# A re-ordered step table for chunked attention followed by a phase-mixing layer, on one core

## The chip, the core and the metric

The kernel runs on one core of a Trainium2 chip. The time is the device time of one execution in microseconds (us), the median over the runs; the profile is one profiled execution of the same program, with its span from the first to the last instruction. The engines are named as the profile names them: PE is TensorE, DVE is VectorE, ACT is ScalarE, POOL is GpSimd and SP is SyncE. PEld is the weight-load half of PE.

## What is computed

Eight batch elements, each of 8 heads, 576 rows and 64 columns per head, go through two stages.

```python
# 1: attention inside chunks of 64 rows
scores = scale * q_c @ k_c.T;  attn = softmax(scores);  x = attn @ v_c      # x: 8 x 576 x 512
# 2: phase mixing and a channel layer
theta = x @ w_theta
zr, zi = x * cos(theta), x * sin(theta)
y = w_tok_r @ zr + w_tok_i @ zi          # over the 576 rows
u = x + y
out = u + relu(u @ w_ch)
```

Inputs and output are float32; inside, the operands of PE are float16 and the sums float32.

## The kernel before, in words

The eight batch elements are worked in four pairs p = 0 to 3. A pair has five groups: A and B are rows 0 to 255 and 256 to 511 of its first element, C and D the same of its second, and M the last 64 rows of both, one in each half of the partitions. A, B, C and D hold two tiles of 128 rows each, M one. A pair thus has nine tiles j = 0 to 8 (A: 0, 1; B: 2, 3; C: 4, 5; D: 6, 7; M: 8).

The work is cut into 562 steps, and the table ORDER writes their order out by hand; every engine executes its own instructions in exactly that order, and waits where an operand or a buffer isn't there yet. A step is named by its kind, the pair and the group or tile, and the buffer or bank that it takes: `S.2B.6` makes the scores of pair 2, group B, in the PSUM bank 6 and the one behind it. The kinds that matter here, with their lines:

- `qk`, `v`, `lw`, `lp`, `lc` are loads, nearly all issued by POOL (L174, L179, L233, L243, L246, L249). They also turn float32 into float16.
- `T`, `Tq`, `Tk` turn q and k on DVE (L286); `S` is the score product on PE (64 small matmuls for a group of two tiles, 32 for M, L325); `E` is the exponential on ACT (L355); `V0`, `V1` are the two halves of the value product on PE (16 small matmuls each, 8 for M, L389); `N0`, `N1` divide by the row sums on DVE (L404, L406).
- `X` transposes x on PE (L421); `xa`, `xv`, `xd` bring it to SBUF by ACT, by DVE, or do the whole transposing by a DMA on SP's queue (L433); `H` is theta on PE (L449); `G` takes cosine and sine on ACT (L471, L472), with a table load (L152) where the exponential was before; `Z` multiplies on DVE (L498, L499).
- `Y` is the token mixing, nine matmuls of 512 columns for a tile on PE (L528); `Ya`, `Yb`, `Ym` are its parts; for the second element of a pair the parts need `Z` of C, of D and of M. `A` adds x on DVE (L550). `U` with `ua` or `uv`, or the DMA `ud` (L563), transposes u. `W` is the channel product on PE (L573), `R` the relu and add on DVE (L578), `st`, `sa`, `sg` are the stores from SP's, ACT's and POOL's queue. `dm` is a filler product of zeros.

The score product uses PE in quarters of 32 rows, the value product in halves of 64; the others use the full array. `crossed(p, g)` says for which groups the second tile's two chunks change sides between the score's rows and the halves of PSUM; `load_v` puts the rows of v where the value product then expects them.

```python
def crossed(p, g):
    return int(p > 0 or g not in "AB")
```

The bank and buffer numbers in the table matter as well: a step that takes a bank waits until the reader of what was in it is done.

Of the kernel before, what the change touches and what calls it, by code (L numbers as in the profile page):

```python
# [23 lines left out]
Z0.0B Ya.01.6 Yb.01 TW.02.4 twa.02 Z.0M Ym.01 T.1M.2 A.01 Yb.03 V0.0C.0 Ym.03 V1.0C.4 Tq.0D.1
S.1M.6 E.1M.4 Ya.02.7 Yb.02 Ym.02 N1.0C Tk.0D S.0D.4 N0.0C A.03 TW.00.0 qk.1B.2 A.02 X.0C.3
lw.04.0 E.0D.3 U.01.6 ua.01.0 U.02.4 ua.02.1 U.03.5 twv.00 Ya.00.0 V1.0D.6 uv.03.2 qk.1A.6
xv.0C.1 N1.0D V0.0D.4 H.0C.2 G.0C.1 qk.1D.3 V0.1M.6 N0.0D X.0D.4 xv.0D.3 v.1B N0.1M Z.0C Yb.00
v.1A Ym.00 v.1D H.0D.4 Ya.05.2 T.1B.4 G.0D.5 V1.1M.3 A.00 Ya.06.6 TW.04.0 S.1B.4 Ya.04.7 N1.1M
X.1M.3 E.1B.4 Z.0D Yb.06 T.1A.4 Ym.06 S.1A.4 qk.1C.6 A.06 Yb.05 T.1D.5 xv.1M.3 U.06.6 twv.04
E.1A.1 Ym.05 Ya.07.4 V1.1B.0 qk.2M.3 A.05 ua.06.3 N1.1B V0.1B.5 N0.1B Yb.04 lc.00 S.1D.2 v.1C  # L30
V1.1A.0 Yb.07 qk.2C.5 Ym.07 qk.2D.4 N1.1A E.1D.2 V0.1D.2 N0.1D X.1B.0 xa.1B.4 V1.1D.5 Ym.04
H.1M.1 H.1B.2 qk.2B.0 N1.1D V0.1A.5 A.07 qk.2A.2 qk.3B.1 Y.08.4 T.1C.7 A.04 N0.1A X.1A.5 U.04.6
G.1M.2 Z.1M xv.1A.1 U.00.7 S.1C.0 v.2M G.1B.6 E.1C.4 A.08 X.1D.5 xv.1D.2 v.2B W.06.2 R.06.3
U.07.0 H.1A.4 uv.04.3 V0.1C.2 v.3D uv.07.4 v.2A uv.00.5 W.00.7 G.1A.7 N0.1C U.05.0 U.08.6
uv.08.5 v.2C V1.1C.2 W.01.1 uv.05.6 H.1D.4 N1.1C X.1C.2 Z.1A Z.1B R.01.2 qk.3A.6 W.08.3 xa.1C.4
Y.10.0 H.1C.1 G.1D.7 Z.1D T.2M.8 T.2A.7 W.02.4 S.2M.5 v.3B G.1C.9 Z.1C R.02.4 E.2M.1 Y.13.6 A.13
T.2B.9 S.2A.1 W.04.4 R.00.0 Y.16.5 qk.3D.0 R.04.5 R.08.6 W.05.4 S.2B.6 T.2D.7 E.2B.7 T.2C.2
Y.11.3 A.11 R.05.8 A.16 W.03.6 R.03.9 Y.15.7 A.15 E.2A.10 V1.2A.5 A.10 S.2C.3 E.2C.11 V0.2M.1
N0.2M V1.2M.7 N1.2M Y.14.2 N1.2A V0.2B.3 N0.2B V0.2A.0 V0.2C.6 v.2D Y.17.5 A.14 A.17 V1.2C.2
N1.2C N0.2A N0.2C Y.18.4 xd.2C.12 S.2D.2 st.04 qk.3M.2 V1.2B.0 E.2D.1 X.2A.5 W.07.6 N1.2B v.3C  # L40
V0.2D.0 R.07.7 N0.2D V1.2D.2 xa.2A.11 v.3A X.2M.7 X.2B.5 v.3M Y.12.6 A.12 N1.2D H.2A.0 xa.2M.10
A.18 T.3A.7 H.2M.6 xa.2B.1 G.2M.13 T.3D.5 Z.2M H.2C.4 H.2B.6 G.2A.6 xd.2D.5 ud.16.4 G.2C.0 Z.2C
ud.17.2 T.3B.9 H.2D.0 W.17.4 S.3D.2 G.2D.4 Z.2D ud.11.6 W.11.5 R.17.5 R.11.13 sa.06 ud.14.3
W.16.0 st.08 qk.3C.8 T.3M.4 Y.25.1 T.3C.1 Y.24.5 Y.27.4 A.24 ud.13.1 G.2B.5 S.3B.5 A.25 W.14.1
R.14.3 Y.26.7 Z.2A S.3M.1 E.3B.6 E.3D.1 V1.3D.2 R.16.12 S.3C.5 A.27 Z.2B sa.07 ud.15.2 ud.12.6
ud.10.4 ud.18.5 W.18.0 E.3C.10 E.3M.7 Y.20.4 sa.17 A.26 V0.3M.7 R.18.11 V0.3C.0 N1.3D W.15.5
R.15.5 N0.3C st.14 S.3A.2 E.3A.3 W.12.6 Y.23.5 V1.3M.2 A.20 N0.3M N1.3M W.10.7 st.11 R.10.7
sa.10 R.12.13 V0.3D.3 N0.3D V1.3C.1 ud.25.3 N1.3C Y.28.0 W.13.4 st.16 ud.27.0 V1.3A.2 V0.3B.6
A.28 st.18 R.13.7 N1.3A Y.21.0 A.21 st.02 ud.24.2 Y.22.2 A.22 xd.3M.12 H.3M.0 V1.3B.3 sa.03
W.24.2 N0.3B N1.3B V0.3A.6 N0.3A ud.20.1 G.3M.10 W.25.1 xd.3D.9 H.3D.3 G.3D.7 xd.3C.1 Z.3M  # L50
H.3C.6 G.3C.5 Z.3D A.23 Z.3C ud.21.4 xd.3B.6 W.21.0 ud.22.3 sa.05 H.3B.3 G.3B.7 Z.3B ud.26.2
W.22.6 st.12 Y.34.7 R.25.8 W.26.3 R.24.6 sg.25 R.22.13 Y.35.1 A.35 R.26.1 R.21.8 xd.3A.10 W.27.6
W.20.2 H.3A.3 sg.21 st.01 st.00 Y.36.0 Y.37.1 R.20.0 sa.20 A.34 ud.28.4 W.28.7 ud.23.6 G.3A.7
A.36 Z.3A Y1.31.0 sa.13 Y.38.3 ud.34.3 A.37 ud.35.1 R.28.7 A1.31 st.24 A.38 W.34.0 Y0.31.7 A0.31
sg.22 ud.37.0 W.37.3 W.35.7 R.34.13 R.37.6 st.26 Y.32.0 A.32 U0.31.3 uv0.31.1 R.35.1 U1.31.1
Y.33.4 A.33 st.15 ud.36.4 W.36.7 W.23.3 R.27.5 ud.38.2 sg.35 sa.34 R.23.13 R.36.1 W.38.6 R.38.0
sa.37 sa.28 Y.30.4 Wp.31.6.7 uv1.31 sa.38 A.30 W0.31 ud.32.3 W.32.1 R0.31.7 sa0.31 R.32.6 U.30.6
sa.36 W1.31 uv.30.1 R1.31 st.27 ud.33.6 W.33.4 R.33.0 st.32 sa.33 W.30.6 sg.23 dm.2.7 R.30.13
st1.31 sa.30
""".split()  # L60


@with_exitstack
def kernel(
# [150 lines left out]
    def crossed(p, g):  # L215

        return int(p > 0 or g not in "AB")
# [64 lines left out]
    def size(g):  # L282
        return 1 if g == "M" else 2
# [464 lines left out]
```

## Time and profile before

| | |
|---|---|
| time, median of 3 runs | 194.83 us |
| all runs | 194.83, 194.02, 199.41 us |
| profiled execution: span from first to last instruction | 191.7 us |
| PE busy | 173.9 us (91%) |
| DVE busy | 138.8 us (72%) |
| ACT busy | 81.4 us (42%) |
| POOL busy | 88.4 us (46%) |
| DMA | 31.86 MB, mean 166 GB/s |

The profiled execution has no time of its own beside its span; the median of the runs lies 3.1 us above the span, the fastest run 2.3 us.

A busy engine is one with an instruction in flight; times count from the start of the span. PE's timeline lists when each matmul starts, so the distance from one start to the next tells what a matmul costs while others follow, and a longer distance than usual is a wait or a change between kinds of matmul. A row of the waits names who waited for whom, the total, how often, and the longest.

### The profile page before, as it was taken

To read this page: it belongs to the slowest core of one execution; us is meant where nothing else is said; L and a number is where in the kernel's file an instruction comes from. 1 tells how busy PE (TensorE), PEld (TensorE's weight loads), DVE (VectorE), ACT (ScalarE), POOL (GpSimd) and SP (SyncE) were. 2 spreads that over 40 slices of the span, in tenths; PEclk is the share of its full clock that TensorE was granted. 3 is DMA by queue.
4 is the path that set the end of the run, shared out by engine and by line. 5 is a ranking of instruction groups with operands and counts; after the bars stand their busy time and mean duration, and the time that the engine had idled before them with its cause. 6 is when DMAs were issued, how large, how long until landed. Compare 5 with 4: busy or idle time off the path is not lost.

```text
span 191.7 us, 5957 instructions
## 1 busy us (share of the span) xinstructions
PE 173.9 (91%) x2579; PEld 91.1 (48%) x2579; DVE 138.8 (72%) x255; ACT 81.4 (42%) x100; POOL 88.4 (46%) x125
## 2 busy tenths in 40 slices
PE   0168899999999999999999969999999999999992
PEld 0155455645554655554555425454444444455450
DVE  0564789879779977996885968396686677553782
ACT  3113895476629946803218659142032560400000
POOL 8998289697798955799878000000000001100110
PEclk9999999999999999999999999999999999999999
DMA  5999999999999999999999986497356894885667
GB/s 159 202 157 182 188 132 143 164 177 165 151 153 183 175 182 181 157 116 152 164 133 132 196 145 168 82 197 222 74 158 126 112 281 103 246 230 150 180 173 259
DMA packets 103338, 31.86 MB, mean 166 GB/s; under 512 B 94672, under 2 KB 99152, under 8 KB 103312
## 3 DMA queue, kind: packets, MB, share of 16 engines
q0 software_dynamic: 76048, 17.33, 98.2%
q1 hardware_dynamic: 23872, 9.57, 23.9%
q10 hardware_dynamic: 3392, 4.59, 7.6%
q8 instruction: 20, 0.33, 0.7%
q14 instruction: 6, 0.05, 0.1%
HBM read 33.06 MB, written 9.44 MB: 222 GB/s over the span
## 4 chain that ended last, share of the span: by engine, by line
PE 78%; DMA 8%; DVE 4%; POOL 4%; issue 2%; ACT 1%; DVEq 0%; ACTq 0%; POOLq 0%
PE psum L528 35%; PE psum L573 14%; PE psum L449 12%; PE psum L325 6%; PE psum L389 5%; DMA out_dram<-mid 3%; PE psum L421 3%; DMA mid<-x 2%; DMA v<-in_v_dram 2%; PE psum L264 1%; POOL big L174 1%; PE psum L555 1%; POOL big L179 1%; DVE mid L578 1%; DVE x L406 1%
## 5 line engine op out<-in xcount | busy, mean ns | idle before, releaser
L528 PE MATMUL psum<-zr,wT 128*128 128x512 f16 (+2 forms) x185 | 62.6, 375 | 0.1
L528 PE MATMUL psum<-zi,wT 128*128 128x512 f16 (+2 forms) x184 | 59.6, 374 | 0.0
L528 PEld LDWEIGHTS <-wT 128*128 128x128 f16 (+1 forms) x369 | 31.3, 100 | 32.9 <-issue 0.5
L233 POOL DMA_DIRECT2D v<-in_v_dram x54 | 41.0, 787 | 10.1 <-DMA big<-in_k_dram 4.5
L672 POOL DMA_DIRECT2D out_dram<-mid x5 | 2.7, 551 | 75.3 <-DVE mid L578 75.3
L573 PE MATMUL psum<-wch,uT 128*128 128x512 f16 x140 | 35.1, 380 | 0.0
L550 DVE TENSOR_TENSOR x<-psum,x 128x512 f16<-128x512 f32 x35 | 23.7, 683 | 15.3 <-PE psum L528 15.1
L449 PE MATMUL psum<-wtheta,mid 128*128 128x512 f16 x144 | 33.2, 379 | 1.7 <-DMA mid<-x 1.7
L355 ACT ACTIVATE mid<-psum 128x1024 f16<-128x1024 f32 (+1 forms) x19 | 17.3, 930 | 33.9 <-PE psum L325 32.2
L578 DVE SCALAR_TENSOR_TENSOR mid<-psum,x 128x512 f32<-128x512 f32 (+1 forms) x37 | 23.9, 669 | 7.7 <-PE psum L573 5.6
L406 DVE TENSOR_TENSOR x<-psum,recip 128x512 f16<-128x512 f32 (+1 forms) x40 | 25.5, 638 | 1.4
L286 DVE STREAM_TRANSPOSE big<-big 128x1024 f32<-128x1024 f32 (+3 forms) x25 | 24.7, 1011 | 1.3 <-DMA big<-in_q_dram 0.9
L325 PE MATMUL psum<-big 32*64 32x64 f16 x1152 | 15.3, 199 | 9.5 <-DVE big L286 9.5
L471 ACT ACTIVATE big<-psum,pihalf 128x1024 f16<-128x1024 f32 x14 | 15.6, 1116 | 17.4 <-PE psum L449 17.4
L449 PEld LDWEIGHTS <-mid 128*128 128x128 f16 x144 | 13.9, 98 | 18.1 <-DMA mid<-x 2.2
L325 PEld LDWEIGHTS <-big 32*64 32x64 f16 x1152 | 13.0, 112 | 15.1 <-DVE big L286 10.1
L573 PEld LDWEIGHTS <-uT 128*128 128x128 f16 x140 | 12.4, 98 | 13.4 <-issue 0.8
L152 ACT ACT_TABLE_LOAD x12 | 15.4, 1283 | 6.3 <-DVE recip L404 4.8
L179 POOL DMA_DIRECT2D big<-in_q_dram x15 | 13.8, 920 | 1.7 <-DMA big<-in_k_dram 0.9
L472 ACT ACTIVATE big<-psum 128x1024 f16<-128x1024 f32 x14 | 14.3, 1024 | 0.0
L389 PEld LDWEIGHTS <-mid 64*64 64x64 f16 x576 | 8.9, 113 | 11.4 <-issue 9.0
L389 PE MATMUL psum<-v,mid 64*64 64x65 f16 x576 | 12.2, 202 | 2.0 <-DMA v<-in_v_dram 1.3
(51 smaller groups left out, 135.7 us busy)
## 6 DMA issues: line engine op xcount, KB each, us to landing
big<-in_q_dram POOLq DMA_DIRECT2D x15, 256.0 KB, 6.5
big<-in_k_dram POOLq DMA_DIRECT2D x15, 256.0 KB, 7.0
out_dram<-mid SPq DMA_DIRECT2D x13, 256.0 KB, 2.8
out_dram<-mid ACTq DMA_DIRECT2D x13, 256.0 KB, 3.0
v<-in_v_dram POOLq DMA_DIRECT2D x18, 128.0 KB, 5.7
v<-in_v_dram POOLq DMA_DIRECT2D x36, 64.0 KB, 6.1
out_dram<-mid POOLq DMA_DIRECT2D x5, 256.0 KB, 3.1
out_dram<-mid SPq DMA_DIRECT2D x5, 128.0 KB, 3.0
```

The source lines that it names most:

```text
L179: nc.gpsimd.dma_start(t[:, w].rearrange("p h s d -> p h (s d)"), ap[2 * p + bb, :, s0 : s0 + GT, :].rearrange("h (p s) d -> p h (s d)", s=2),)
L233: nc.gpsimd.dma_start(v16[rows, slot + t, :, 0:D], v[b, :, t0 : t0 + m, :].rearrange("h s d -> s h d"),)
L286: nc.vector.transpose(out.bitcast(FP32).rearrange("p (x l s) -> p x s l", l=32, s=2), in_.bitcast(FP32).rearrange("p (x s d) -> p x s d", ...
L325: nc.tensor.matmul(ps[half[to], r, h], t[quarter[c], 1, h, :, e], t[quarter[c], 0, h, :, e], start=(e == 0), stop=(e == 1), tile_position= ...
L355: nc.scalar.activation(out=eT[:, 0:n].rearrange("p r h i -> p (r h i)"), in_=st.pop(("ps_s", p, g)).rearrange("p r h i -> p (r h i)"), fun ...
L389: nc.tensor.matmul(ps[half[cc], r, h4, :], eT[rows, r, h, :], v16[rows, slot + r, h, 0 : D + 1],)
L406: nc.vector.tensor_tensor(out=x.rearrange("p r (h d) -> p r h d", h=HH), in0=ps[:, :, :, 0:D], in1=recip[:, 0:n].broadcast_to((P, n, HH, D ...
L449: nc.tensor.matmul(ps, xT[:, a, :], wtheta16[:, a, :], start=(a == 0), stop=(a == NDB - 1))
L528: nc.tensor.matmul(ps[half[b]] if j == MID else ps, w, z[:, cols], start=(kt == 0), stop=(kt == 2 * KT),)
L550: nc.vector.tensor_tensor(out=x, in0=st.pop(("ps_y", p, j)), in1=x, op=ALU.add)
L573: nc.tensor.matmul(ps, uT[:, a, :], wch16[:, a, :], start=(a == 0), stop=(a == NDB - 1))
L578: nc.vector.scalar_tensor_tensor(out=out, in0=ps, scalar=0.0, in1=x, op0=ALU.max, op1=ALU.add)
```

## The change

The table has the same 562 steps, for twelve of which another engine does the copying (fewer on DVE, more on ACT), and for sixteen another queue the store. The words of the change say that the order came from a search whose model holds TensorE at each block of 256 instructions until its read could have come; no instruction in the program does that.

The order of the steps up to `Z0.0B` is the one before, with other buffers and banks. Behind it the steps are placed anew:

- On PE the small products (`S`, `V`) stand in fewer and longer rows. PE passes from a small product to a full-size one or back 73 times in the table before, and 47 times now; inside such rows it passes between `S` and `V` 10 times before, 6 now. The number of matmuls of each kind is the same (2579 in all).
- In the load order the first difference is behind `v.1B`: `v.1D` stands ahead of `v.1A`, and then `v.2M`, `v.2D`, `qk.3M` come much earlier, `qk.2D`, `qk.2C`, `qk.2B` later.
- Some stores and DMA transposes (`sa.05`, `st.04`, `ud.13`, `ud.15`, `ud.11`, `xd.2D`) stand ahead of the last loads.

In the code, `crossed` becomes `turned`, so that in groups B and D the first tile changes sides in place of the second, with the loads of v split accordingly (one load of 128 rows and two of 64, as before). The score function can take two groups at once (`SS`), which no step of the new table uses. A half step takes its buffer where it has a number, not where it is the first half.

Three places show how instructions move. In the rows, L numbers are each file's own: the change's L286, L326, L397, L429, L447, L506, L507, L536, L558, L581, L586, L613 and L638 are L286, L325, L389, L421, L439, L498, L499, L528, L550, L573, L578, L605 and L630 before.

The first place is DVE behind theta of pair 0, group C, where group D of pair 0 and the first groups of pair 1 follow. Before:

```order
L439 COPY mid<-psum 128x1024
L404 RECIPROCAL recip<-psum 128x4
L406 TENSOR_TENSOR x<-psum,recip 128x256
L498 TENSOR_TENSOR zr<-x,big 128x1024
L499 TENSOR_TENSOR zi<-x,big 128x1024
L286 STREAM_TRANSPOSE big<-big 128x16x2x32
```

With the change:

```order
L447 COPY mid<-psum 128x1024
L506 TENSOR_TENSOR zr<-x,big 128x1024
L507 TENSOR_TENSOR zi<-x,big 128x1024
L286 STREAM_TRANSPOSE big<-big 128x16x2x32
L558 TENSOR_TENSOR x<-psum,x 128x512
L286 STREAM_TRANSPOSE big<-big 128x16x2x32
L506 TENSOR_TENSOR zr<-x,big 128x1024
L507 TENSOR_TENSOR zi<-x,big 128x1024
L286 STREAM_TRANSPOSE big<-big 128x16x2x32
L558 TENSOR_TENSOR x<-psum,x 128x512 x2
```

The copy of x of group D comes first in both; now `Z.0C`, `T.1B`, `A.00`, `T.1A`, `Z.0D` and `T.1D` follow with no division between them, since the value product of 1M has moved behind the scores of 1A, 1B and 1D.

The second place is PE around the scores of pair 2, group B. Before, they stand alone between a channel and a mixing product:

```order
L573 LDWEIGHTS uT
L573 MATMUL psum<-wch_70,uT 128x512
L325 LDWEIGHTS big
L325 MATMUL psum<-big 64x64
...
L528 LDWEIGHTS wT
L528 MATMUL psum<-zr,wT 128x512
```

With the change, three score products (`S.3M`, `S.3B`, `S.2B`) and half a value product (`V1.2C`) follow each other, 352 instructions (each matmul and each weight load is one) between the last mixing matmul and the transposes:

```order
L536 LDWEIGHTS wT
L536 MATMUL psum<-zr,wT 128x512
L326 LDWEIGHTS big
L326 MATMUL psum<-big 64x64
...
L397 LDWEIGHTS mid
L397 MATMUL psum<-v_72,mid 64x65
...
L429 LDWEIGHTS x
L429 MATMUL psum<-id_65,x 128x128
```

Two more such rows are new: `S.2M`, `S.2D`, `S.2A` (320 instructions) and `S.1A`, `S.1B` (256). The longest before, behind the start, has 224 (`S.3M`, `V1.3D`, `S.3C`).

The third place is the end of DVE's program. Before:

```order
L578 SCALAR_TENSOR_TENSOR mid<-psum,x 128x512 x4
L630 COPY uT<-psum 128x256
L550 TENSOR_TENSOR x<-psum,x 128x512
L578 SCALAR_TENSOR_TENSOR mid<-psum,x 128x256
L578 SCALAR_TENSOR_TENSOR mid<-psum,x 128x512
L565 COPY uT<-psum 128x512
```

With the change:

```order
L613 TENSOR_TENSOR x<-psum,x 128x256
L586 SCALAR_TENSOR_TENSOR mid<-psum,x 128x512 x7
L638 COPY uT<-psum 128x256
L586 SCALAR_TENSOR_TENSOR mid<-psum,x 128x512 x2
L638 COPY uT<-psum 128x256
L586 SCALAR_TENSOR_TENSOR mid<-psum,x 128x512 x4
L586 SCALAR_TENSOR_TENSOR mid<-psum,x 128x256 x2
```

All additions of x are done first, and thirteen full relu steps (`R`) with two half ones close the program; the last tile is the halved one, 31, and no longer 30.

The diff, cut to its core:

```diff
 ORDER = """
-H1.0A.5 G1.0A.0 H1.0B.0 G1.0B.3 xv.0M.4 Tq.0C.2 Z1.0A H0.0A.7 qk.0D.0 lw.00.6 G0.0A.1 v.0D
+H1.0B.7 G1.0B.6 xv.0M.7 Tq.0C.11 Z1.0A H0.0A.4 qk.0D.12 lw.00.14 G0.0A.8 v.0D twv.03 Z0.0A H.0M.0
 ...
-    def crossed(p, g):
-
-        return int(p > 0 or g not in "AB")
+    def turned(p, g, r):
+
+        if p == 0 and g in "AB":
+            return 0
+        return r ^ int(g in "BD")
 ...
-        elif not crossed(p, g):
-            parts = [(slice(0, P), t, 2 * p + bb, s0 + t * P, P) for t in range(2)]
         else:
-            parts = [
-                (slice(0, P), 0, 2 * p + bb, s0, P),
-                (half[1], 1, 2 * p + bb, s0 + P, CH),
-                (half[0], 1, 2 * p + bb, s0 + P + CH, CH),
-            ]
+            parts = []
+            for t in range(2):
+                t0 = s0 + t * P
+                if turned(p, g, t):
+                    parts += [(half[1 - i], t, 2 * p + bb, t0 + i * CH, CH) for i in range(2)]
+                else:
+                    parts.append((slice(0, P), t, 2 * p + bb, t0, P))
 ...
-    def score_mms(ps, t, n, heads, cross):
+    def score_mms(groups, n, heads):
         for h in range(heads):
             for e in range(2):
                 for c in range(2 * n):
+                    for p, g, ps, t in groups:
 ...
-                    to = cc ^ (r * cross)
+                        to = cc ^ turned(p, g, r)
 ...
-                        rows = half[cc ^ (r * crossed(p, g))]
+                        rows = half[cc ^ turned(p, g, r)]
```

More of the change, by code (lines that the diff above doesn't have):

```diff
@@ L24 @@
[L24 to L41, printed above, removed]
```

104 lines of the change are left out of this document (62 added, 42 removed).

## The prediction, made before the changed kernel ran

> **What bounds the kernel now.** I read the page first, for the engine that has no room left.
>
> ```profile
> PE 173.9 (91%) x2579; PEld 91.1 (48%) x2579; DVE 138.8 (72%) x255; ACT 81.4 (42%) x100; POOL 88.4 (46%) x125
> PE   0168899999999999999999969999999999999992
> DMA  5999999999999999999999986497356894885667
> ```
>
> PE is busy in nearly every slice from the fourth to the last but one; one 6 stands at about 110 us. Since a busy PE need not be a fast one, the waits of PE come next, and then the windows.
>
> ```profile
> PE psum L325 <- DVE big L286: 9.5, 2, 9.0
> PE psum L449 <- DMA mid<-x: 1.7, 1, 1.7
> PE psum L389 <- DMA v<-in_v_dram: 1.3, 2, 0.7
> PE psum L421 <- DVE x L406: 0.9, 1, 0.9
> PE psum L389 <- ACT mid L355: 0.7, 1, 0.7
> ...
> 40.00:104.00 64.00, 64.00 (x1164) 34.16 (x1163) 53.60 (x98) 34.49 (x42) 52.59 (x70) 1.00 1.87 158
> ```
>
> The first row is the start, while q and k come in and are turned; the third, fourth and fifth lie ahead of 20.2 us as well. From there to the end PE waits once that counts, 1.7 us for a DMA transpose. In 64 us of the middle it has no gap. So the span is made of three parts: the time until PE gets going, PE's own stream, and a tail. The stream is looked at by the distances between starts, from PE's timeline:
>
> ```profile
> 80.45 0.38 PE L528 MATMUL psum<-zi,wT 128*128 128x512 f16 x1
> 80.67 0.38 PE L528 MATMUL psum<-zr,wT 128*128 128x512 f16 x1
> 80.97 0.71 PE L325 MATMUL psum<-big 32*64 32x64 f16 x64
> 81.61 0.60 PE L573 MATMUL psum<-wch,uT 128*128 128x512 f16 x2
> ...
> 90.57 0.38 PE L528 MATMUL psum<-zi,wT 128*128 128x512 f16 x1
> 90.88 0.32 PE L389 MATMUL psum<-v,mid 64*64 64x65 f16 x16
> 91.13 0.71 PE L325 MATMUL psum<-big 32*64 32x64 f16 x64
> ...
> 94.19 0.58 PE L389 MATMUL psum<-v,mid 64*64 64x65 f16 x48
> 94.71 0.39 PE L528 MATMUL psum<-zr,wT 128*128 128x512 f16 x1
> ```
>
> A full-size matmul costs 0.22 us (80.45 to 80.67). On the way into a small product it costs 0.30 or 0.31 (80.67 to 80.97, 90.57 to 90.88): 0.09 more. 16 small value matmuls take 0.25 with the way out, 48 take 0.52; so 32 more cost 0.27, 16 cost 0.13, and 0.12 is the way out of a small kind, to a full-size product (94.71) as to another small one (91.13). A row of small products between two full-size ones thus costs 0.21 beside its work.
>
> **The change, part by part.** *The stream.* 73 passages between small and full-size are 36.5 such rows, 47 are 23.5: 13 x 0.21 = 2.7 us less. Four fewer passages between the two small kinds at 0.12 are 0.5 less. The matmuls are the same. PE's stream is 3.2 us shorter.
>
> *The gate at 38.9 us.* Not all of that comes through, since the loads set the pace first. From the timelines of DVE, POOL and PE, and the DMA issues of 30.4 to 34.2 us:
>
> ```profile
> 34.49 0.71 DVE L286 STREAM_TRANSPOSE big<-big 128x512 f32<-128x512 f32 x1 [0.26 <-DMA big<-in_k_dram]
> ...
> 30.46 3.69 POOL L233 DMA_DIRECT2D v<-in_v_dram x5
> ...
> v<-in_v_dram POOLq DMA_DIRECT2D x4, 64.0 KB, 6.5
> ...
> 38.61 0.38 PE L528 MATMUL psum<-zi,wT 128*128 128x512 f16 x1
> 38.92 0.45 PE L389 MATMUL psum<-v,mid 64*64 64x65 f16 x32
> ```
>
> DVE waits for k of group 0D and turns it from 34.49; five loads of v are issued in 3.69 us from 30.46, the third of them, the last of v.0D, at about 32.0 and with 6.5 us to landing at 38.5. The value product of 0D starts at 38.92: loads and PE arrive together. The change leaves POOL's loads in their order up to there, the DMA is full (9 in every slice of the page's row), and so this product can't start earlier, by my reckoning at 38.9. Priced by the distances above, PE has 147.5 us of stream left at that point before, and 146.1 with the change: only 1.4 of the 3.2 us come behind the gate, the rest (less the few matmuls that have moved behind it) turns into waits ahead of it, at the scores of 0D and here.
>
> *The wait of 1.7 us* goes. It is for the transpose of x of group 2D, which starts 4.7 us before PE needs it is over; the chain shows it:
>
> ```profile
> 107.49 4.72 DMA mid<-x
> ...
> 112.26 1.90 PE psum L449 x8
> ```
>
> In the new table this transpose is issued behind the division of 2D, some 102 us by the stream's count, and wanted at about 110. With 4.72 us it is there at 107, and the one of 2C is issued at about 108 and wanted at 115. Nothing replaces the wait here. If the cover were gone, it would cost 1.7 again.
>
> *The tail.* PE's last matmuls before, and the end of the chain:
>
> ```profile
> 187.55 0.59 PE L163 MATMUL psum<-zeros 128*128 128x512 f16 x2
> 187.30 1.29 DVE L578 SCALAR_TENSOR_TENSOR mid<-psum,x 128x512 f32<-128x512 f32 x2 [0.36 <-DMA out_dram<-mid]
> ```
>
> PE is through at 187.8 and the span ends at 191.7: 3.9 us for the last relu and its store, which the change has as well (two half relus at the end, 0.42 each, in place of whole ones). So PE's end is 38.9 + 146.1 = 185.0, the span's 188.9. But DVE now has fifteen relus in one go. They follow each other every 0.64 us (1.29 for two, of which the last part overlaps), PE makes the products at 0.86; the second of them waits for `W.23`, whose product ends at 176.4 by PE's count. Six whole ones (3.8), two copies of 0.22, six more (3.8) and two halves (0.8) from there end at 185.3, where PE alone would let them end at 185.0: 0.3 more.
>
> *DVE and ACT between 39 and 53 us.* The new order packs the first place of the listing tightly. Prices, by form:
>
> ```profile
> L286 DVE STREAM_TRANSPOSE big<-big 128x1024 f32<-128x1024 f32 x12 | 14.5, 1224 | 0.1
> L499 DVE TENSOR_TENSOR zi<-x,big 128x1024 f16<-128x1024 f16 x14 | 9.6, 689 | 1.2 <-ACT big L472 1.1
> L550 DVE TENSOR_TENSOR x<-psum,x 128x512 f16<-128x512 f32 x35 | 23.7, 683 | 15.3 <-PE psum L528 15.1
> L152 ACT ACT_TABLE_LOAD x12 | 15.4, 1283 | 6.3 <-DVE recip L404 4.8 <-PEq L732 1.3
> L355 ACT ACTIVATE mid<-psum 128x1024 f16<-128x1024 f32 x15 | 15.1, 1020 | 32.1 <-PE psum L325 32.0
> ```
>
> DVE is free behind the copy of 0D at 43.1; `Z.0C` (2 x 0.69), `T.1B` (1.22), `A.00` (0.68) and `T.1A` (1.22) end at 47.6, while PE asks for `S.1A` at 47.4: 0.3 of wait with the way there. On ACT the sine of 0D ends at 47.4, then come a copy (0.65), a table load with its dummy (1.5), `E.1B` and `E.1A` (1.02 each) and `E.1M` (0.6), over at 52.2 to 52.7, while PE wants `V0.1M` at 52.3 to 52.6: 0.4. Below, these are nothing, if PE is held elsewhere first; above, one whole turn or exponential each, 2.2. I take 0.7.
>
> *Blocks of instructions.* This the trace shows only from the side. PE's program is read in blocks while it runs:
>
> ```profile
> q8 instruction: 20, 0.33, 0.7%
> ...
> 0.00:93.30 93.30, 80.75 (x1525) 45.74 (x1526) 72.06 (x135) 50.91 (x65) 75.98 (x107) 1.00 1.75 164
> 0.00:95.90 95.90, 83.35 (x1582) 47.04 (x1583) 74.18 (x140) 50.91 (x65) 78.02 (x110) 1.00 1.75 164
> q8 instruction: 1, 0.02, 5.9%
> ...
> 0.00:81.29 81.29, 68.74 (x1294) 39.52 (x1298) 61.65 (x119) 47.67 (x62) 64.56 (x92) 1.00 1.71 168
> 0.00:150.50 150.50, 136.27 (x2379) 72.90 (x2380) 114.53 (x214) 73.41 (x92) 85.63 (x120) 1.00 1.46 158
> ```
>
> 20 reads of 0.33 MB are 16 KB each, for 5158 instructions one to each 256. By 93.30 PE had 3051 instructions (1525 + 1526), just under 12 blocks, and the read comes only at 95.9 (its 5.9% of 16 engines in the 1.1 us from there are 1.0 us): landed 3.6 us behind the border. One comes at 81.29, with 2592 begun, 32 behind the border of 2560, some 0.2 us: landed by about 1.7, if it takes somewhat longer than the other. One comes at 150.5, with 4759 begun, 105 ahead of the border of 4864: PE's sequencer is ahead of PE where full-size matmuls run. If a block has to be there one border later, what counts is the time between borders. Before, they lie over 4 us apart. With the change, I count from the table 1.4 us (`S.3B`, `S.2B`, `V1.2C`), 2.0 us (`S.2D`, `S.2A`), and 2.9 and 3.3 us around 1A, 1B and 1D. With reads of 1.7 us only the first is short, by 0.3. With 3.6 us all are, by 2.2, 1.6, 0.7 and 0.3: 4.8. Below nothing, if reads run ahead. I take 1.0, nearer to the fast reads, since all four rows of small products follow full-size matmuls.
>
> [...]
>
> *Nothing* comes of `turned` and of the split of v: the same number of matmuls, and of loads of the same sizes. Twelve copies that change engines lie on ACT or DVE beside PE's stream, and DVE has 4 fewer of them; if PE waited for them, one costs 0.4 to 1.0.
>
> *The sum*: 188.9 + 0.3 + 0.7 + 1.0 = 190.9 us of span, 0.8 less than 191.7. The median of the runs lies 3.1 above the span, so 194.0.
>
> **The rivals.** *All holds vanish.* PE runs on from the gate as it did before in 64 us without a gap: 188.9 of span, 192.0. For it speaks that the new table leaves DVE and ACT no more work than before; against it the 0 to 0.3 us of room that I find at six places.
>
> *The reads decide.* If each block lands 3.6 us behind its border, as the one at 95.9 did, PE stands at four places for 4.8 us in place of 1.0: 190.9 + 3.8 = 194.7 of span, slower than before, 197.8. It turns slower than before once the four places cost over 1.8. Against it: in the trace no wait of PE is at a border, though that is with borders 4 us apart.
>
> *The loads fall behind.* Three stores and three or four DMA transposes now run before the last loads. From the queue rows:
>
> ```profile
> q10 hardware_dynamic: 3392, 4.59, 7.6%
> ```
>
> 7.6% of 191.7 us for 4.59 MB, ACT's queue with its stores, are 3.2 us a MB, 0.8 for a store of 256 KB. Three of these and four transposes at no more than that are 5.6 us; v of 2B has by the load order some 4.5 to 8 us to spare. At the worst 1.1 us late, and up to 2 if v slows down: 192.9 of span, 196.0.
>
> *The order changes nothing that counts*: the loads still set the gate, and a new wait of 1.7 us replaces the old: 190.6 and 193.7, inside my own range.
>
> **How the numbers follow.** My forecast has 0.50, with a range of its own from 192.3 to 195.7 (the terms of DVE, ACT and the reads from nothing to twice); the order that changes nothing, 0.05 beside it. All holds vanish: 0.18. The reads: 0.13. The loads: 0.08. The last 0.06 are for waits that I haven't seen. The range from 190.6 to 198.0 holds these, with 1.4 below the second for the tail and for the scatter of the runs (194.02 to 199.41 before). A measurement of this kernel can tell about 2% from no change, 3.9 us: faster than 190.9 needs the second case and luck, 0.10; slower than 198.7 needs the worst of the reads or an unseen wait, 0.09; the rest is 0.81.
>
> **What would show it.** Right: the value product of 0D near 38.9 us, waits at the scores of 0D before it, no wait of theta for a transpose in pair 2, PE through at 185 to 187, and the small gaps where I put them. Wrong: a start of that product over 1 us earlier, which would mean that the loads don't set it; gaps of over 1 us inside the three long rows of small products (reads); waits of PE for v or for DVE's turns between 80 and 110 us (loads); or a tail of over 5 us.

## The result, and the profile after

| | before | after |
|---|---|---|
| median of the runs | 194.57 us (4 runs, 194.02 to 199.41) | 208.61 us (4 runs, 206.39 to 210.03) |
| ratio | | 1.069, 95% interval 1.060 to 1.078: slower |
| profiled execution, span | 191.7 us | 206.3 us (its own time 208.05) |
| PE begins its last matmul | 187.8 us | 196.4 us |
| from there to the end of the span | 3.9 us | 9.85 us |
| last load landed | 111.2 us | 124.7 us |

Ratios here and below compare only runs within 1.5% of the fastest run of their kernel; the 199.41 and 210.03 us of this table and the profiled runs of c2 and c4 lie above that.

The span is 14.6 us longer: 8.7 until PE's last matmul and 5.9 behind it. The page of the changed kernel shows where to look. First PE's busy time, then PE, its granted clock and the DMA engines in the 40 slices of 5.16 us:

```profile
PE 173.5 (84%) x2579; PEld 92.5 (45%) x2579; DVE 135.7 (66%) x251; ACT 84.5 (41%) x104; POOL 89.1 (43%) x126
PE   0168998999799999979973996999999999999910
PEclk9999999999999999999998899999999999999995
DMA  6999999999999999999999999033765751348995
```

PE's busy time is the same, but its row now has a 7 in the slices at 52 and 88 us, a 7 and a 3 from 103 to 113, a 6 at 124, and a 1 and a 0 at the end. The DMA row is full up to 129 us (25 slices) instead of 110 (23 of 4.79), then drops to nothing, and is full again at the end. The waits of PE (who waits, for whom, total, times, longest):

```profile
PE psum L326 <- DVE big L286: 10.5, 3, 9.0
PE psum L326 <- issue: 5.9, 2, 4.7
PE psum L536 <- issue: 1.5, 1, 1.5
PE psum L397 <- DMA v<-in_v_dram: 1.3, 2, 0.6
PE psum L457 <- DMA mid<-x: 1.2, 1, 1.2
...
PE psum L581 <- DMA uT<-x: 0.7, 1, 0.7
```

Rows two and three are new: "issue" is a wait for nothing that another engine did. PE's timeline (start, length, line, count, and in brackets the idle time ahead) has the three places:

```profile
52.15 0.44 PE L397 MATMUL psum<-v,mid 64*64 64x65 f16 x24
54.12 0.38 PE L536 MATMUL psum<-zr,wT 128*128 128x512 f16 x1 [1.52 <-issue]
...
87.16 1.48 PE L326 MATMUL psum<-big 32*64 32x64 f16 x129
89.91 0.44 PE L326 MATMUL psum<-big 32*64 32x64 f16 x31 [1.27 <-issue]
...
105.40 1.72 PE L326 MATMUL psum<-big 32*64 32x64 f16 x134
111.77 0.58 PE L326 MATMUL psum<-big 32*64 32x64 f16 x26 [4.66 <-issue]
```

Two of them stand in the middle of a row of identical score products, `S.2A` and `S.2B`; the third is ahead of `Ya.05`. Counted in PE's program (weight loads and matmuls), PE stops there at instructions 1724, 2748 and 3516. All three leave the remainder 188 when divided by 256. The three distances between starts are 1.7, 1.5 and 4.85 us: 8.0 together. The trace has the transfers of the instruction queue singly as well; the one for the last of these places is

```profile
q8 instruction: 1, 0.02, 6.1%
```

in the window from 109.44 to 110.38 us. PE entered the block before at 105.49 (instruction 3260), the read started at 109.45 and landed at 110.37, and PE went on at 111.77. For the other two the landings are 52.57 and 88.40; PE went on 1.55, 1.51 and 1.40 us behind the landing. The read of `S.2A` was quick: PE had entered the block before at 87.16, the read landed 1.2 us later, just as PE came to the border. Its 1.5 us are the going on alone. A fourth new row, `S.3D` and `S.3C` with 256 instructions at 133.5 us, is not held; the read for the border in it had landed at 126.2.

Behind the last hold PE is slow for a while. In the windows the column of the granted clock is the one behind POOL's count:

```profile
104.00:112.30 8.30, 3.64 (x171) 2.56 (x169) 2.35 (x5) 1.62 (x2) 3.80 (x5) 0.95 1.83 184
112.30:116.00 3.70, 3.70 (x60) 1.87 (x60) 1.92 (x4) 2.51 (x3) 0.68 (x1) 0.66 1.46 186
116.00:130.00 14.00, 11.93 (x101) 5.40 (x87) 11.50 (x21) 8.16 (x9) 0.00 (x0) 1.00 1.46 139
```

From 111.41 the clock is granted at half for 3.41 us, and the products of `W.13` take 0.43 us instead of 0.22: with the small products ahead of them, some 1.2 us.

Then come two waits for DMA transposes (`H.2C` 1.33, `W.14` 0.84) and one for a bank that DVE still reads (`W.16` 0.31), and last the tail, in ACT's timeline:

```profile
188.41 0.59 ACT L575 COPY uT<-psum 128x512 f16<-128x512 f16 x1 [21.44 <-PE psum L563]
188.42 11.71 ACTq L680 DMA_DIRECT2D out_dram<-mid  x7
200.22 1.29 ACTq L687 DMA_DIRECT2D out_dram<-mid  x1
```

ACT stands 21.4 us at the copy `ua.30`, which needs the transpose `U.30`. Seven stores and the last half one are queued behind that copy, among them `sa.06` of pair 0, whose tile had been done for over 100 us, and go out only from 188.4 on.

The account of PE, by the distance of each step's start from a stream without stalls: shorter stream -3.2, the old wait of `H.2D` -1.8, waits at the gate (`TW.02` for its load, `S.0D` for its turn) +1.6, the three holds +8.0, the half clock +1.2, transposes and the bank +2.5: +8.3 of the +8.7; the rest is not traced to single places.

### The profile page after: what moved, and what is told of

The parts are those of the page before. It is cut to its first block, busy times and chain, and to the rows that moved or that the text cites. A ratio compares the mean times of both kernels' runs of the same rounds, so it can differ in the third digit from the quotient of the medians.

```text
span 206.3 us, 5953 instructions
## 1 busy us (share of the span) xinstructions
PE 173.5 (84%) x2579; PEld 92.5 (45%) x2579; DVE 135.7 (66%) x251; ACT 84.5 (41%) x104; POOL 89.1 (43%) x126
## 2 busy tenths in 40 slices
DMA packets 103338, 31.86 MB, mean 154 GB/s; under 512 B 94672, under 2 KB 99152, under 8 KB 103312
## 4 chain that ended last, share of the span: by engine, by line
PE 67%; DMA 11%; POOL 8%; issue 5%; DVE 2%; SPq 1%; ACT 1%; DVEq 0%; POOLq 0%
PE psum L536 32%; PE psum L581 14%; PE psum L457 11%; DMA big<-in_k_dram 5%; PE psum L326 4%; POOL v L233 4%; DMA uT<-x 3%; DMA big<-in_q_dram 3%; PE psum L397 3%; PE psum L429 2%; POOL big L177 1%; PE psum L563 1%; POOL big L172 1%; DVE x L558 1%; SPq L571 1%
## 5 line engine op out<-in xcount | busy, mean ns | idle before, releaser
L536 PE MATMUL psum<-zr,wT 128*128 128x512 f16 (+2 forms) x185 | 61.9, 375 | 1.5 <-issue 1.5
L536 PE MATMUL psum<-zi,wT 128*128 128x512 f16 (+2 forms) x184 | 59.5, 374 | 0.0
L536 PEld LDWEIGHTS <-wT 128*128 128x128 f16 (+1 forms) x369 | 31.7, 100 | 34.7 <-issue 1.9
L233 POOL DMA_DIRECT2D v<-in_v_dram x54 | 41.1, 779 | 10.6 <-DMA big<-in_q_dram 2.5
L558 DVE TENSOR_TENSOR x<-psum,x 128x512 f16<-128x512 f32 x35 | 23.2, 683 | 20.2 <-PE psum L536 20.1
L457 PE MATMUL psum<-wtheta,mid 128*128 128x512 f16 x144 | 33.7, 379 | 1.4 <-DMA mid<-x 1.2
L581 PE MATMUL psum<-wch,uT 128*128 128x512 f16 x140 | 34.0, 387 | 0.9 <-DMA uT<-x 0.7
L326 PE MATMUL psum<-big 32*64 32x64 f16 x1152 | 15.1, 200 | 16.5 <-DVE big L286 10.5
L286 DVE STREAM_TRANSPOSE big<-big 128x1024 f32<-128x1024 f32 (+3 forms) x25 | 25.2, 1018 | 4.5 <-DMA big<-in_q_dram 3.0
L586 DVE SCALAR_TENSOR_TENSOR mid<-psum,x 128x512 f32<-128x512 f32 (+1 forms) x37 | 23.6, 670 | 6.6 <-PE psum L581 6.6
L326 PEld LDWEIGHTS <-big 32*64 32x64 f16 x1152 | 13.2, 113 | 20.9 <-DVE big L286 11.6
L581 PEld LDWEIGHTS <-uT 128*128 128x128 f16 x140 | 13.4, 100 | 17.2 <-issue 2.0
L150 ACT ACT_TABLE_LOAD x12 | 15.4, 1283 | 1.5 <-PEq L740 1.3
L177 POOL DMA_DIRECT2D big<-in_k_dram x15 | 13.8, 918 | 2.7 <-DMA big<-in_k_dram 2.4
L449 ACT COPY mid<-psum 128x1024 f16<-128x1024 f16 (+1 forms) x8 | 7.7, 961 | 15.1 <-PE psum L429 15.0
```

Source lines behind the costliest of these rows:

```text
L177: nc.gpsimd.dma_start(t[:, w].rearrange("p h s d -> p h (s d)"), ap[2 * p + bb, :, s0 : s0 + GT, :].rearrange("h (p s) d -> p h (s d)", s=2),)
L233: nc.gpsimd.dma_start(v16[rows, slot + t, :, 0:D], v[b, :, t0 : t0 + m, :].rearrange("h s d -> s h d"),)
L286: nc.vector.transpose(out.bitcast(FP32).rearrange("p (x l s) -> p x s l", l=32, s=2), in_.bitcast(FP32).rearrange("p (x s d) -> p x s d", ...
L326: nc.tensor.matmul(ps[half[to], r, h], t[quarter[c], 1, h, :, e], t[quarter[c], 0, h, :, e], start=(e == 0), stop=(e == 1), tile_position= ...
L457: nc.tensor.matmul(ps, xT[:, a, :], wtheta16[:, a, :], start=(a == 0), stop=(a == NDB - 1))
L536: nc.tensor.matmul(ps[half[b]] if j == MID else ps, w, z[:, cols], start=(kt == 0), stop=(kt == 2 * KT),)
```

## The experiments

The theory, an estimate from these three holds and from the 20 reads of 0.33 MB, one to each 256 instructions: PE comes no further than the next border until the read that starts behind its entry into a block has landed (at the three it started 0.2 to 4.0 us behind that entry and landed 1.2 to 4.9 behind it), and goes on 1.40 to 1.55 us behind the landing. That the read is asked for at the entry, and lies behind the loads in the DMA until it starts, is my assumption; no view shows it. Beside it: transfers ahead of the last loads make transposes late, and stores queued behind `ua.30` make the tail. Rivals were the code (`turned`, the loads of v), a shortage of buffers or late turns that only look like holds, and an order that loses the time anyway.

**c1, the code alone.** The table of before in the changed code.

```diff
-ORDER = """ (the new table)
+ORDER = """ (the table of before)
```

> The code of the change (the other side changed in groups B and D, the loads of v split accordingly) with the step table of before. Theory: the code costs nothing, all of the loss comes from the order: span 191 to 193 us, as before. Rival: the other sides or the new order of the two v loads of 64 rows cost something: over 194.

Measured: 194.90 us (8 runs) against 194.30, ratio 1.003 (0.998 to 1.009), span 192.5. The code costs nothing; it is all in the table.

**c2, the borders shifted.** 64 tiny products of zeros, 128 instructions, in a gap ahead of `X.0B`, at 20 us.

```diff
+dq.64.5
 X.0B.5
```

> The changed kernel with 64 tiny score-sized matmuls of zeros (128 instructions) put where PE waits 0.85 us at about 19 us; they move every border of 256 instructions by half a block against the work. Theory (PE stands at block borders until a read is there): the holds move with the borders, to the middle of S.1D (near 51.7 us), into V0.2A (near 94), into S.3B (near 106) and to V0.2C, and no hold is left behind V0.1B, in S.2A and in S.2B; in sum 6 to 9 us, span 204 to 208. Rival (the holds belong to operands or buffers of those products): they stay at Ya.05, S.2A and S.2B with 1.5, 1.3 and 4.7 us.

Measured: 209.5 and 214.2 us; the profile is of the run of 214.2, with a span of 212.4 (the other has 207.8). PE runs through all three old places. It stops at seven new ones, `S.1D` 0.5, `X.1M` 2.2, `S.1C` 0.6, `V0.2A` 1.6, `V1.2D` 0.5, `S.3B` 1.9 and `V0.2C` 3.4 us, and each of these is again at remainder 188. The four longest:

```profile
63.40 0.27 PE L433 MATMUL psum<-id,x 128*128 128x128 f16 x2 [2.02 <-issue]
99.50 0.39 PE L401 MATMUL psum<-v,mid 64*64 64x65 f16 x25 [1.41 <-issue]
113.53 1.28 PE L330 MATMUL psum<-big 32*64 32x64 f16 x90 [1.67 <-issue]
121.65 0.78 PE L401 MATMUL psum<-v,mid 64*64 64x65 f16 x38 [3.19 <-issue]
```

Together the seven are 10.7 us, more than the 6 to 9 that I expected, and three of them stand where I had named none. But neither banks nor turns can move with 128 instructions of zeros: the holds belong to the count of instructions.

**c3, five stores early.** The five steps leave their old places.

```diff
 G.3A.18
+sa.06 sa.11
 ...
 st.08
+st.17
 ...
 R.28.13
+st.27 st.28
```

> The changed kernel with five stores that wait in the queues until the end (tiles 6, 11, 17, 27, 28) placed right behind the point where their tiles have long been finished. Theory (the tail of 9.7 us is the stores that are left when PE ends): 1.25 MB less at about 310 GB/s, tail 5 to 6 us, span about 202. Rival (the tail is set by the late relus of the last tiles): tail stays over 9, span 206.

Measured: 203.6 us (2 runs), ratio 1.049 (1.018 to 1.081), span 202.8. PE's last matmul starts at 196.5 as before, and the tail is 6.3 us instead of 9.85. The holds stay at 1.5, 1.1 and 4.8 us. So 3.5 of the 5.9 us of longer tail were these stores, two of them from behind `ua.30`; six more still stand there. What the two and the three of SP's queue are worth singly was not measured.

**c4, the rows taken apart.** Here too the steps are moved.

```diff
+Ya.05.4 Yb.05 Ym.05
 S.1D.5
 ...
 S.2D.6
+W.01.5
 S.2A.2
 ...
+S.3M.7
 Y.16.0
 S.3B.4
+Y.12.1
 S.2B.2
```

> The changed kernel with full-size products put between the small ones in its three long rows (W.01 between S.2D and S.2A; Y.16 and Y.12 between S.3M, S.3B and S.2B; Ya.05, Yb.05 and Ym.05 ahead of S.1D). Theory (block reads): 256 instructions then take 5.7, 2.3 and 5.6 us in place of 3.7, 1.3 and 1.4; the holds of 1.7, 1.5 and 4.9 us fall to 0, 0.4 and 0.8, and with them the 0.9 us of half-speed matmuls behind the longest: PE ends 6 to 8 us earlier, span about 199. Rival (the holds are waits for loads that come late): PE waits as long, at the value products of 2B, span 205 or more.

Measured: 205.5 and 208.6 us; the profile is of the run of 208.6, with a span of 206.9. The holds are gone but for 0.2 us in `S.2A`. PE's last matmul starts at 197.0 all the same, and not 6 to 8 us earlier. `S.3M`, moved ahead, took a bank that DVE had not read yet and waited 3.0 us, half clock was granted for 6.8 us from 102.4, and `H.2D` and `H.2C` waited 1.7 and 2.7 us for transposes. The place of the gain was taken at once, in part by my own move.

**c5, fewer loads.**

```diff
 def load_v(p, g):
+    if p == 3:
+        return
```

> The changed kernel with the loads of v of pair 3 left out (2.36 of 31.86 MB; the value products of pair 3 then use pair 1's v). Theory: the block reads and the DMA transposes come late because the loads, which now end at 124.7 us instead of 111.2, share the DMA engines with them. Then, with v.3B and v.3A gone ahead of it, the read for the block entered in S.3M lands 3 to 4.3 us behind the border instead of 4.9 and the hold inside S.2B shrinks from 4.85 to 3 to 4.3 us; the loads end near 113 to 117 us; the waits of H.2C (1.33), W.14 (0.84) shrink to 0.8 us together or less. Rival (the reads are late by a time of their own, and the transposes wait on their own queue): the hold stays at 4.85 within 0.3 us and the two waits stay at 2.2 us together within 0.4. The times of the first two holds (1.75, 1.47) stay in both.

Measured: 202.7 us, span 200.9, PE's last matmul at 191.1. The hold in `S.2B` falls from 4.85 to 1.8 us, below the range that I gave, and `H.2C` and `W.14` don't wait any more. The last load landed at 102.8 us, well ahead of the 113 to 117 that I expected. So this row ran with no load in flight, though with stores and transposes, and was held all the same:

```profile
105.40 1.76 PE L328 MATMUL psum<-big 32*64 32x64 f16 x134
108.79 0.41 PE L328 MATMUL psum<-big 32*64 32x64 f16 x26 [1.62 <-issue]
```

Its read landed 1.8 us behind the entry into the block, and the next border was 1.5 us away. The loads are then some 3 of the 4.85 us. For the transposes, the DMA issues of 95 to 113 us tell more (kind, count, size if any, median us from issue to landing); first the changed kernel, then c5:

```profile
uT<-x SPq DMA_TRANSPOSE x5, 8.5
mid<-x SPq DMA_TRANSPOSE x1, 11.9
```

```profile
uT<-x SPq DMA_TRANSPOSE x5, 4.4
mid<-x SPq DMA_TRANSPOSE x1, 4.8
```

In c5 the two that were issued at 97.4 and 99.3, with loads still in flight, took 7.4 and 6.4 us; those issued from 103.6 on took 3.3 to 4.8.

**c6 and c7, a long row made on purpose**, in the kernel before: while loads are in flight, and when none are.

```diff
+dq.128.2
 S.2D.2
```

```diff
+dq.128.6
 W.22.6
```

> The kernel before with 128 tiny products of zeros (256 instructions, 1.25 us of PE) added just ahead of S.2D at 99 us, while loads are in flight; they begin at instruction 3238, so a block is entered 22 instructions later and the next one 256 instructions, some 1.3 us, behind that. Theory (a block's read goes out as the block before it is entered, lands 1.9 to 5.3 us later while loads are in flight, and PE goes on 1.45 us behind the landing): a hold of 2 to 5.5 us at instruction 3516, inside S.2D, that PE's own sequencer ends, and none elsewhere; span 194.5 to 199 us. Rival (long rows cost nothing by themselves; the holds of the changed kernel are the sequencer's waits for something else): no hold over 0.3 us there, span 193 to 193.5.

> The kernel before with the same 128 tiny products just ahead of W.22 at 154.6 us, when no loads are in flight; they begin at instruction 4796, at the border itself, so that the next one is 1.25 us behind. Theory (the lag of the read is that of transfers queued ahead of it): the read has landed ahead of the border as in the kernel before (2.8 us ahead there), the hold is 0 to 0.5 us, span 192.7 to 193.5. Rival (256 instructions in 1.25 us are a hold wherever they stand, since a read and the going on alone take 1.0 and 1.45 us): a hold of 1.2 us or more at the next border.

Measured: no hold at the row in either (198.3 and 199.3 us). Neither told anything about a short interval, since the row was slow: all its products use the same quarter of PE and one place of PSUM and took 32 ns each, so that the borders were 3.7 and 4.0 us apart, and the reads came 2.1 and over 7 us ahead of the next one. Elsewhere PE does stand at borders in these two, 1.1 us at 65.9 in c6 and 0.4 at 102.5 in c7, though nothing was changed there. They showed something else, too: in c6, PE has no gap around the row, and yet

```profile
99.00:104.30 5.30, 5.30 (x165) 4.58 (x162) 2.03 (x5) 0.00 (x0) 5.29 (x7) 1.00 1.72 115
104.30:107.70 3.40, 3.40 (x90) 2.26 (x78) 0.90 (x2) 2.04 (x2) 0.00 (x0) 0.50 1.54 207
```

the clock is at half for 3.4 us behind it (PE's busy time equals the window in both rows, the granted clock is 1.00 and then 0.50). In c7 the same happens at 159.1.

**c10 and c11, the same with a fast row**, its products spread over the four quarters and four places of PSUM, as the score product's are.

```diff
+dq.140.2
 S.2D.2
```

```diff
+dq.140.3
 H.3B.3
```

> The kernel before with 140 tiny products of zeros ahead of S.2D at 99 us, now spread over the four quarters of PE as in the score product, since the earlier ones, all in one quarter, took 29 ns each and left 3.74 us between the two borders (they were no test of a short interval). 22 instructions to the border, 258 behind it; at the 10 ns of the score product the next border is 1.3 us behind. Loads are in flight. Theory: a hold of 1.5 to 5 us at instruction 3516, ended by PE's own sequencer. Rival (long rows cost nothing by themselves): none over 0.3 us.

> The same 140 products ahead of H.3B at 153 us in the kernel before, when no loads are in flight (16 instructions to the border, 264 behind it). Theory (the lag is that of transfers queued ahead of the read, so that away from the loads it has come in time): a hold of 0 to 0.5 us at instruction 5052. Rival (256 instructions in 1.3 us are a hold anywhere, since a read takes 1 us and the going on 1.45): 1 us or more.

Measured: 199.8 and 195.5 us, with the kernel before at 194.1. PE's timeline in c10, and in c11:

```profile
99.45 1.31 PE L170 MATMUL psum<-zeros 32*64 32x64 f16 x137
103.31 0.22 PE L170 MATMUL psum<-zeros 32*64 32x64 f16 x3 [2.54 <-issue]
```

```profile
153.80 1.54 PE L170 MATMUL psum<-zeros 32*64 32x64 f16 x140
155.27 1.04 PE L459 MATMUL psum<-wtheta,mid 128*128 128x512 f16 x4
```

With loads in flight the row is held 2.7 us at instruction 3512 (the read landed at 102.06), and half clock follows for 6.8 us; a second hold of 1.7 us stands at 3768, one block on. Without loads 140 products go through in one piece though the borders are 1.24 us apart: there the read had started at 151.6 and landed at 152.5, before the block ahead of it was entered (153.8). So a long row by itself need not be held. That it never is without loads isn't shown: this is one place, where the read ran 2.2 us ahead. In the kernel before, the reads behind the last load landed between 2.8 us ahead of that entry and 2.2 us behind it, and in c5 the row was held 1.8 us behind the end of the loads.

**c8, all of it mended**: c3's stores; `Ya.05`, `Yb.05`, `Ym.05` and `W.01` as in c4; and the third row as follows (PE's steps alone).

```diff
 Y.16.0
 S.3M.7 S.3B.4
+Y.12.1
 V1.2C.0 X.2M.6 W.13.7 W.15.6
+S.2B.2
 V0.2C.4
+H.2M.7 W.16.4 W.18.5
 V1.2B.0 V0.2B.2
```

> The changed kernel with the five deferred stores early (as measured alone: tail 6.1 instead of 9.7 us) and the three crowded rows taken apart without a product that is moved ahead of its bank's reader: Ya.05, Yb.05, Ym.05 ahead of S.1D; W.01 between S.2D and S.2A; and in the third, S.3M and S.3B, then Y.12, V1.2C, X.2M, W.13, W.15, and S.2B only then (with H.2M, W.16, W.18 ahead of V1.2B). The two borders there are then 5.75 us apart instead of 1.43, against 6.3 us that the late read needed. Theory: the holds are gone but for 0 to 1 us in S.2B, no half clock follows, PE ends 8 to 9 us earlier than the changed kernel's 196.65 (188 to 189), tail 5 to 6.5: span 193 to 195.5, time 195 to 197.5, within 2% of before. Rival (the stalls only move: whatever waits for loads, banks or transposes takes the place of the holds): PE ends at 193 or later, time 201 or more.

Measured: 205.7 us (4 runs), ratio 1.058 (1.053 to 1.063), span 205.6, PE's last matmul at 199.5. The rival holds. The holds are 0.6 and 1.4 us instead of 8.0, and PE lost more than that elsewhere:

```profile
PE psum L457 <- DMA mid<-x: 3.8, 1, 3.8
PE psum L429 <- DVE x L414: 2.9, 2, 2.0
PE psum L326 <- issue: 1.6, 2, 1.2
```

`H.2C` now waits 4.2 us, until 127.6; in the changed kernel it started at 125.4. The time of `H.2C` is set by its transpose, which was issued at 117.0 and took 10.6 us among the late loads. Its issue was late by PE's own pace, though: SP's queue stood 2.7 us for it until the value product of 2B had freed its buffer.

**c9, two transposes by PE.** c8's order without those DMA transposes, and with `T.2B`, `ud.11`, `X.2M`, `W.13`, `W.16` placed anew.

```diff
-xd.2D.8
-xd.2C.7
+X.2D.3 xa.2D.8
 V1.2C.0
 ...
+X.2C.7 xv.2C.7
 X.2B.1
```

> The mended order, with the x of 2D and of 2C transposed by PE (X.2D, X.2C, with a copy on ACT and on DVE) in place of the two DMA transposes on SP's queue, whose results came at 118 to 127.5 us, and with T.2B, ud.11, W.16 and X.2B a place or two later where the mended order had made waits of 0.9 to 2.2 us of its own. It costs PE some 1.0 us for the two products. Theory (from 113 us on PE waits for DMA transposes that stand behind the late loads): the wait of 4.21 us in H.2C and the half clock behind it (0.9) go, and the two waits of 2.15 and 1.25 fall to 1 us together; PE ends at 190.5 to 193.5 instead of 199.5, span 196.5 to 200, time 198 to 202. Rival (the last loads themselves are what PE then waits for, through the turns of 3D and 3C on DVE): PE ends at 196 or later.

Measured: 206.1 us (2 runs), ratio 1.065 (1.048 to 1.082), PE's last matmul at 197.2. The wait of `H.2C` is gone, and 3.8 us stand at `X.2C`: its bank waits for `G.2M`, `G.2M` for a buffer, the buffer for the store `sa.00`, issued at 112.3 and landed at 120.4. Again a transfer among the last loads, of another kind. The hold in `S.2B` was 2.7; here PE went on 2.7 us behind the landing of the read, later than at the three holds of the changed kernel (1.40 to 1.55), and why is open.

**c12 and c13, the six stores left out** (`sa.05`, `st.04`, `sa.03`, `sa.00`, `st.01`, `st.02`) of the changed kernel and of c9.

```diff
-sa.05
-st.04
-sa.03
-sa.00
-st.01
-st.02
```

> The changed kernel without the six stores that stand ahead of the last loads (sa.05, st.04, sa.03, sa.00, st.01, st.02: 1.57 MB, some 9 us of transfer at 170 GB/s; these six tiles of the output are not written). Theory (the loads end 13.5 us later because stores and transposes were put ahead of the last of them, and block reads and transposes are late with them): the loads end at 115 to 119 us instead of 124.7; the hold inside S.2B shrinks from 4.85 to 2.5 to 4.3 us; the waits of H.2C and W.14 (1.33 and 0.84) fall to 0.8 us together or less. Rival (it is the late issue of the loads and the transposes; the stores are hidden): loads end at 122 or later, the two waits stay at 1.8 us or more.

> The order of the kernel with X.2D and X.2C on PE, without the same six stores (their tiles are not written). There PE lost 3.83 us at X.2C, whose bank waited for G.2M, whose buffer waited for the store sa.00 to land at 120.5, and 2.67 us at the border inside S.2B. Theory (all that PE lost behind 100 us were the block reads, and buffers and transposes behind crowded transfers): the 3.83 goes, the 2.67 falls to 0.5 to 2, PE ends at 189.5 to 193 instead of 197.2, some 5 us behind that the span: 195 to 198.5. Rival (something else of the order holds PE between 112 and 130 us): PE ends at 195 or later.

Measured: 207.6 and 202.3 us, PE's last matmul at 195.2 and 194.2. In c12 the waits of `H.2C` and `W.14` are gone, as expected; but the loads end at 121.6, not at 115 to 119, and the hold in `S.2B` is 5.1 us, not smaller. So those stores are 3 of the 13.5 us by which the loads are late, and they made the late transposes later: those issued from 118 us on took 3.2 to 4.0 us instead of 7.2 to 8.5, those of 104 to 110 still 7.3 to 11.6. They do not set the lag of the block reads. In c13 the 3.8 us are gone, the hold is 1.85, and PE still ends 1.2 us later than I expected: borders inside `S.3M` and `X.2C` (1.0 each), half clock (1.0), and waits of 0.6 to 0.8 at four places from 31 to 60 us.

**c14, one transpose by PE in the kernel before.**

```diff
-xd.2D.5
 H.2M.6
+X.2D.2 xv.2D.5
 H.2C.4
```

> The kernel before, with x of 2D transposed by PE (X.2D, bank 2, between H.2M and H.2C, copied by DVE ahead of Z.2M) in place of the DMA transpose for which H.2D waits 1.67 us by the releasers (2.26 by the gap). It costs PE 0.45 us of product and 0.1 of passage. Theory (a transpose by DMA is late while loads are in flight, and PE pays for it): H.2D starts without a wait, span 190.2 to 190.9 instead of 191.7, time 0.992 to 0.996 of before. Rival (another late thing takes its place at once: W.17, T.3B or the bank): the span stays at 191.5 to 192.2, ratio 0.998 to 1.002.

Measured: 193.71 us (12 runs) against 193.90, ratio 0.999 (0.996 to 1.002). `H.2D` doesn't wait any more; `W.17` behind it does, 0.7 us, 0.5 of them for its own DMA transpose, and PE pays 0.55 for the product. No gain that can be measured. No version tried here beats the kernel before.

## Why the prediction was wrong, point by point

| term | predicted | measured |
|---|---|---|
| start of the value product of 0D | 38.9 us | 39.04 us |
| PE's stream behind the gate, without stalls | 146.1 us, 1.4 shorter | 145.7 us (157.4 less 11.7 of stalls), 1.3 shorter |
| DVE and ACT, 39 to 53 us | 0.7 | 0, held elsewhere |
| reads of blocks | 1.0 | 8.0, and 1.2 of half clock |
| wait for a transpose in pair 2 | none | 2.2, and 0.3 for a bank |
| tail | 3.9 + 0.3 | 9.85 |
| code (`turned`, loads of v) | nothing | nothing (c1) |

The differences of these rows are together the 15.4 us from the 190.9 us of span that were predicted to the 206.3 measured. The 3.1 us that were put between span and median on top were 1.8 in the profiled run.

**The step that failed is the one on the blocks**: "With reads of 1.7 us only the first is short, by 0.3 … I take 1.0, nearer to the fast reads". It came to 8.0, and to 1.2 of half clock behind them. It failed in three places. First, the border was put at multiples of 256. The stops in c2 and in the changed kernel show it 68 instructions ahead of that. With it, the read at 81.29 us of the kernel before belongs to the border at 78.8 and landed 4.0 us behind it: in that kernel there were no fast reads while loads were in flight. All reads of that part landed 1.9 to 5.3 us behind their borders; only later, without loads, did they come between 2.8 ahead and 2.2 behind. Second, PE went on only 1.40 to 1.55 us behind the landing, which the sum didn't have. So borders there would have to be 3.3 to 6.9 us apart, not 1.7 to 3.6: an estimate, 1.9 and 1.4 at the least, 5.3 and 1.55 at the most. `S.2A` shows this point alone: a read of 1.2 us, quicker than the one that was taken as fast, and still a hold of 1.5. Third, one lag was priced for all four rows, and it is not one number: under loads the reads of the changed kernel landed 1.2 to 6.2 us behind the entry into the block ahead, that of `S.2B` 4.9 (1.8 in c5). That is not more than the kernel before had; there the borders were far enough apart. Its shortest interval was 3.5 us, at 99 us, and not over 4; there the read landed after 1.9, PE came to the border 1.6 us behind the landing, and passed with 0.4 us to spare at most (1.6 less the 1.25 that it took to go on in c10). (In c7 that read came 0.8 us later, and PE stands 0.4 us at this border.) The many short rows of the kernel before cost 3.2 us of PE's stream; what they bought is that distance.

The rival "The reads decide" named this mechanism and the right rows, at 4.8 us and a chance of 0.13. The price was too low for the reasons above, and it got too little weight: the argument against it, "no wait of PE is at a border, though that is with borders 4 us apart", says nothing on borders 1.4 us apart.

**"Nothing replaces the wait here."** The wait of `H.2D` is gone, as forecast, but by luck: its transpose was issued at 107.2, not at 102, took 11.9 us, not 4.72, and landed at 119.0. PE, late from the holds, came to `H.2D` only at 119.7. In c4, without the holds, `H.2D` waits 1.7 us. And the transpose of 2C was issued at 117.65 and not at 108, since PE was late: the division of 2C ended at 117.5, with SP's queue free from 114.3. `ud.14` took

```profile
120.70 7.17 DMA uT<-x
```

7.17 us, against 4.72 for the one that was priced. The rival "The loads fall behind" saw stores and transposes ahead of the last loads, but counted three stores where there are six, and looked for the damage at v of 2B, which was in time; it came through the transposes and, in c9, through a buffer.

**The tail** was priced by DVE's relus alone. What is late is the queue of stores behind a copy that waits: ACT executes in the order of the table, which had put eight stores behind `ua.30`: that copy started at 188.41 us, and the first of them was issued at 188.42. Three lines of the order of ACT would have shown it. c3 measured 3.5 us for two of these and three late ones of SP's queue.

What held: the prices of passages, the gate, and that the code is free. They are 3.2 us of a change whose other parts cost 17.8.

**What stays open.** Why the reads lag is shown only in part. The loads are some 3 us of the longest hold (c5); but under loads a read of 1.2 us occurs, and without them one of 1.8. c10 and c11 differ in the loads and also in a read that ran ahead. Whether it is the number of transfers queued or their bytes was not separated, and c12 shows that six stores less do not change it. Each mended order met a late transfer of another kind between 112 and 128 us, which points to the loads' end at 118 to 128 us as the bound behind the holds, but does not show it: in c8 the transpose waited for PE as well. An order with the new rows and the old order of loads was not tried.

## What to carry to other kernels

Count PE's instructions, weight loads too, in any stretch where small matmuls follow each other while loads are in flight: where 256 of them went by faster than a block's read landed and PE went on behind it (2.75 us from the entry in `S.2A`, 6.28 in `S.2B`), PE stood inside the row here, for 1.5 and 4.85 us. Without loads PE went through borders 1.24 us apart in c11, but c5 had a hold of 1.8 us there too. A forecast that takes one stall away should ask what is late next on the same transfers: here holds, transposes, buffers and stores took each other's place, and removing the largest moved the time by less than its size. An engine that issues stores should not have a copy that waits for the end of the program ahead of them: here eight stores stood behind one until 188.4 us, and two of them, with three of SP's queue, were 3.5 us of the tail.

## What the runs showed of the hardware

- PE stopped at remainder 188 of 256 instructions in the changed kernel (three places) and in c2 (seven), and at 184 in c10 (3512 and 3768). It went on 1.40 to 1.55 us behind the landing of the read in the changed kernel, 1.25 in c10 and 2.7 in c9.
- In c6 the clock went to half behind a row of products in one quarter of PE, without any idle time: 0.50 for 3.4 us, with PE busy in the whole window, so that the waits of PE alone do not show the place. In the changed kernel it was at half for 3.41 us from 111.41, and in c4 and c10 for 6.8 us.
- Tiny products (32 by 64) took 32 ns each in one quarter of PE and one place of PSUM (128 in 4.04 us, in c6 and in c7), and 10 ns spread over four of each (140 in 1.33 us in c11).
- The DMA transposes issued between 95 and 113 us took 8.5 (median of five) and 11.9 us from issue to landing in the changed kernel, and 4.4 and 4.8 in c5, which moves 30.68 MB instead of 31.86.
